# Reordering copies for the transposing DMA: from ScalarE and VectorE to GpSimd

## The chip, the core and the metric

The kernel runs on one core of a Trainium2 chip. A core has a matrix engine (TensorE, PE in the profile; its weight loads are PEld), three engines for elementwise work (VectorE or DVE, ScalarE or ACT, GpSimd or POOL), an engine that mostly issues transfers (SyncE, SP), and 16 DMA engines that move data between the device memory and the on-chip memory SBUF, or within SBUF. Matmuls write into PSUM, here one tile of 8 banks. Each engine works through its own instructions in order and waits on semaphores for the others. The metric is the device time of one execution in microseconds; lower is better.

## What is computed

Attention with a squared ReLU in the place of the softmax, and then a two-layer feed-forward net with a parametric ReLU over the same tokens:

```python
# q, k, v: (8, 12, 448, 64) float32
scores = (1 / sqrt(64)) * q @ k^T
attn   = maximum(scores, 0) ** 2 / 448
x      = (attn @ v).transpose(0, 2, 1, 3).reshape(3584, 768)
h      = x @ w_in                       # w_in: (768, 2048)
g      = maximum(h, 0) + alpha * minimum(h, 0)
out    = g @ w_out                      # w_out: (2048, 768), out: (3584, 768) float32
```

## The kernel before

The work is cut into 24 quads. A quad is four heads of one batch, so there are three quads to a batch (NG = 3); quad n belongs to batch n // 3. The 448 rows of a sequence are taken as 64 times 7: row 7 * pp + j lies on partition pp, and j runs from 0 to 6. On the other 64 partitions lies the second head of a pair, and the index m (called s later) tells two such pairs apart. All tiles that TensorE reads are bfloat16.

A quad goes through these steps:

- **Load.** `load_qk(n)` and `load_v(n)` (L111 to L125) issue one transfer each for q, k and v on GpSimd's queue, which also turns float32 into bfloat16. q and k arrive as raw tiles of 128 partitions by (s, j, d), 896 elements. There are three raw buffers for q, three for k and six for v.
- **Order and turn.** The score matmul needs q and k with the head dimension on the partitions. The first five quads are turned on TensorE (`turn_pe`). From quad 5 on `turn_dma` (L188) does it: two copies (L195), one for q and one for k, put the raw rows from the order (s, j, d) into (j, s, d) in a tile `perm`, and one transposing DMA on SP's queue (L197) makes the tile T of the quad from it. The pool of `perm` has one buffer; that of T has four. For quads 5, 7 and 8 the copies go to the tile `w_mix`, which is not yet in use for its own purpose.
- **Wait and load on.** `prepare(n)` (L408) calls `turn_dma(n)` and then `land(n)` (L417), a copy of one element on GpSimd that reads T. It holds up GpSimd's queue until T(n) is there; behind it stand the loads of q and k for quad n + 2 and of v for quad n + 1.
- **Scores.** For each j, `score_mm` (L209) makes four 64 by 64 matmuls into a pair of PSUM banks. ReLU goes from PSUM to SBUF on ACT (L218) or DVE (L220), the square from SBUF to SBUF on DVE (L231, both inputs the same SBUF tile) or ACT (L229).
- **Attention times v.** `attnv` (L241), 28 matmuls, with the result copied out by ACT (L253) and DVE (L255) into xT.

The feed-forward net runs one batch later. A word f of the plan (`f1_mm`, `f1_out`) is six matmuls over 448 columns (L275) for one of 16 blocks of the hidden dimension, then ACT's negative part (L281) and DVE's combination (L282) into gT. The second layer goes by pairs of 128-row blocks: `Pair` (L315) makes seven products of half size (L335) in the place of eight, with operand sums on DVE (L331, two SBUF inputs, and once L313 for the weights) and output sums on DVE (L340, one input in PSUM); a few blocks go plainly (L300). SP stores the results (L291) out of six output buffers.

There is no scheduler. The order of everything is written out by hand in plans, strings of words that `Walk.step` carries out one by one: f is a block of the first layer, c a chunk of scores with a letter for each ReLU's engine, s a square, v an attention step, p and r steps of a pair, and n the preparation of the next quad. After n stands the engine of its two copies: `nD` is VectorE, a plain `n` is ScalarE. Five plans cover batches 2 to 7; `EACH` serves batches 3, 4 and 6. Plan words that name quads 24 and 25 do nothing. The words n make quads 11 to 23.

Of the kernel before, what the change touches and what calls it, by code (L numbers as in the profile page):

```python
# [20 lines left out]
def kernel(  # L21
# [10 lines left out]
    nc = tc.nc  # L32
    B, H, S, D = q.shape
# [75 lines left out]
    raw, vraw = {}, {}  # L109
# [78 lines left out]
    def turn_dma(n, eng="A"):  # L188
        if n in (5, 7, 8):
            w = w_mix[2 + n % 2].rearrange("p k c -> p (k c)")[:, :4 * NJ * D]  # L190
            p = w.rearrange("p (a j s d) -> p a j s d", a=2, j=NJ, s=2)
        else:
            p = perm_pool.tile([128, 2, NJ, 2, D], BF16, tag="perm", name="perm")
        for i, name in enumerate("qk"):
            (nc.vector.tensor_copy if eng == "D" else nc.scalar.copy)(p[:, i], raw.pop((n, name)).rearrange("p s j d -> p j s d"))  # L195
        t = T_pool.tile([128, 2, NJ, 128], BF16, tag="T", name="T")
        nc.sync.dma_start_transpose(out=t.rearrange("p a j c -> p (a j) c"),  # L197
                                    in_=p.rearrange("p a j s d -> p (a j s d)"))
        T[n] = t
# [208 lines left out]
    def prepare(n, eng="A"):  # L408
        if n < NQ:
            turn_dma(n, eng)  # L410
            land(n)
        if n + 2 < NQ:
            load_qk(n + 2)
        if n + 1 < NQ:
            load_v(n + 1)
# [4 lines left out]
    class Walk:  # L420
# [12 lines left out]
        def step(self, w):  # L433
# [36 lines left out]
            elif c in "pr":  # L470
                if rest[0] in "abcd":
                    getattr(self, c).mix("abcd".index(rest[0]) + 1)
                else:
                    getattr(getattr(self, c), "p" + rest)()
            elif c == "w":
                i, half = int(rest[0]), int(rest[1])
                weight_mix(i, 4 * half, 4 * half + 4)
            elif c == "g":
                f2(self.b // 2, int(rest[0]), int(rest[1]))
            elif c == "n":  # L480
                prepare(self.quad, rest or "A")
                self.quad += 1
            elif c == "x":
                cast0(int(rest[0]), int(rest[1]), rest[2])
            elif c == "t":
                turn_pe(int(rest[0]), ((rest[1], int(rest[2]), int(rest[3]), rest[4]),))
            elif c == "d":
                turn_dma(int(rest[:-1]), rest[-1])
            elif c == "l":
                land(int(rest))  # L490
            elif c == "L":
                n = [int(x) for x in rest[1:].split(",")]
                {"q": load_qk, "v": load_v, "i": load_w_in, "o": load_w_out}[rest[0]](*n)
            elif c == "i":
                warm(int(rest))
            elif c == "z":
                two_queues.append(1)
            elif c == "b":
                nc.vector.tensor_scalar(beta_sb, alpha_sb, -1.0, 1.0, ALU.mult, ALU.add)
# [8 lines left out]
    pairs = {2: (((0, 5), (0, 6)), ((1, 0), (1, 1))), 3: (((1, 2), (1, 3)), ((1, 4), (1, 5))),  # L508
             4: (((1, 6), (2, 0)), ((2, 1), (2, 2))), 5: (((2, 3), (2, 4)),), 6: (((2, 6), (3, 0)), ((3, 1), (3, 2))),
             7: (((3, 3), (3, 4)), ((3, 5), (3, 6)))}  # L510
    FIRST_PAIR = """B f s1A f s2D s0D s1D n f f s0D f f f f s0D cDA cA f s0D s1A nD pa pb r1 f pc s0A f f f f f f p6 r2 cADA s1D v cAA ra s0D pd cA p7 rb n p5 s2D p4 s0D p3 s1A s0A cADA s2A s0D rc r6 v rd cADA s2D r7 r5 s0A s0D cAAD s0A r4 r3 cA v cAA"""
    EACH = """B f s0D f s0A f n f f f f s2A f s1D cAAA s1D f f s0D f s0A f p1 nD f f r1 f f s1A pc p2 pa r2 ra pb cA vDA s1D s0D cAA p6 s0D pd p7 n cA rc s1A cAA s0D s0A p5 p4 rb p3 cAAD v cAD s1D s1A s3A cA s3A r6 s2A r7 rd r5 s0A cAD r4 s0D r3 cAD v cD cA"""
    ONE_PAIR = """B f f nD s2A s0A s2D f s1D f f f s1D f f s0A f f cAD s1D cA s0D n s0D f f f f f f pc pa g50 pb cADA v p1 cAAA s0A p6 s2D s0A p2 pd p7 s1A p5 n s0A p4 p3 s0D cADA s0D v cAD s1A s2A cD s2A s1D g51 s0D cDAD v cD cA cA"""
    LAST = """B f s0A f f f f s3A s2A s2A f f s2A f f f f f f pc f f s0A f p1 r1 pa pb p2 p6 p7 pd ra p5 rb rc p4 p3 r6 z r7 rd r5 r2 r3 r4e"""
    for b, plan in ((2, FIRST_PAIR), (3, EACH), (4, EACH), (5, ONE_PAIR), (6, EACH), (7, LAST)):
        walk.p, walk.r = ([walk.r] if b == 2 else []) + [Pair(*t) for t in pairs[b][b == 2:]] + [None] * (b == 5)
# [31 lines left out]
```

## Time and profile before

| | |
|---|---|
| median of three runs | 372.95 us (372.71 to 373.54) |
| the profiled execution | 373.66 us |
| its span, first to last instruction | 371.9 us |
| mean granted TensorE clock | 0.995 |
| busy: PE, DVE, ACT, POOL | 362.9, 277.9, 274.7, 72.5 us |

The profiled execution is one more run, with its own time; the span is what the profile's rows cover, and 1.8 us lie around it. Busy time counts the union of an engine's instructions, without waits and without the issue of transfers by ACT and SP. [...]

### The profile page before, as it was taken

Reading aid. Unit: us, or ns where it says so; the run is one execution under the profiler, and the core shown is the slowest. Engines: PE = TensorE matmul, PEld = TensorE weight load, DVE = VectorE, ACT = ScalarE, POOL = GpSimd, SP = SyncE. Lnnn points to the kernel's source line nnn. Section 1 sums busy time; section 2 is a strip of 40 time slices with the busy share of each in tenths; the row PEclk is TensorE's granted clock in tenths of the full one; section 3 lists DMA queues with packets and bytes.
Section 4 is the critical chain, followed back from the end, with each engine's and each line's share of the span. In section 5 each row is a group of like instructions: output and inputs, shape, how many; then the busy total and the mean of one; then the engine's idle time right before and its main releaser. Section 6 shows DMA issues by size and latency. Waiting matters only on the chain.

```text
span 371.9 us, 7878 instructions
## 1 busy us (share of the span) xinstructions
PE 362.9 (98%) x3097; PEld 196.7 (53%) x3097; DVE 277.9 (75%) x445; ACT 274.7 (74%) x406; POOL 72.5 (19%) x120
## 2 busy tenths in 40 slices
PE   7799999999999999999999999999999999999996
PEld 5454564445454565545555455554555455555563
DVE  3989988885968989566887668888849667856653
ACT  4998676877997678885897859967699866964400
POOL 8567150304113222021020220202200000000000
PEclk9899999999999999999999999999999999999999
DMA  9999979998999878455882558727647201220024
GB/s 145 193 204 202 196 120 187 159 167 148 183 173 141 119 118 156 102 85 92 156 150 64 96 81 167 143 59 121 101 95 136 50 2 43 65 65 0 0 64 108
DMA packets 73557, 43.29 MB, mean 116 GB/s; under 512 B 40368, under 2 KB 73008, under 8 KB 73520
## 3 DMA queue, kind: packets, MB, share of 16 engines
q0 software_dynamic: 27136, 22.58, 42.0%
q1 hardware_dynamic: 45712, 19.61, 26.1%
q10 hardware_dynamic: 672, 0.59, 0.5%
q8 instruction: 24, 0.39, 0.4%
q14 instruction: 13, 0.11, 0.1%
HBM read 45.62 MB, written 11.01 MB: 152 GB/s over the span
## 4 chain that ended last, share of the span: by engine, by line
PE 91%; ACT 3%; DVE 2%; DMA 1%; issue 1%; ACTq 0%; DVEq 0%; POOLq 0%
PE psum L275 38%; PE psum L335 30%; PE psum L209 8%; PE psum L241 8%; PE psum L300 6%; DMA kraw<-in_k_dram 1%; ACT rl L218 1%; PE psum L183 1%; DVE gT L282 1%; ACT xT L253 1%; ACT neg L281 1%; DVE w_mix L195 1%; DVE at L231 0%; DVE T L186 0%; DVE osb L340 0%
## 5 line engine op out<-in xcount | busy, mean ns | idle before, releaser
L275 PE MATMUL psum<-xT,w_in_sb 128*128 128x448 bf16 x768 | 150.4, 353 | 0.3 <-DVE gT L282 0.2
L282 DVE SCALAR_TENSOR_TENSOR gT<-neg,beta_sb,psum 128x448 bf16<-128x448 f32 x128 | 85.2, 679 | 43.4 <-ACT neg L281 42.1
L218 ACT ACTIVATE rl<-psum 128x896 bf16<-128x896 f32 x128 | 111.1, 924 | 7.2 <-PE psum L209 5.2
L275 PEld LDWEIGHTS <-w_in_sb 128*128 128x128 bf16 x768 | 73.4, 98 | 73.2 <-issue 6.7
L281 ACT ACTIVATE neg<-psum 128x448 f32<-128x448 f32 x128 | 68.5, 547 | 41.0 <-PE psum L275 32.7
L231 DVE TENSOR_TENSOR at<-rl 128x896 bf16<-128x896 bf16 x105 | 62.1, 618 | 0.5 <-ACT rl L218 0.2
L229 ACT ACTIVATE at<-rl 128x896 bf16<-128x896 bf16 x63 | 58.5, 951 | 0.3
L335 PEld LDWEIGHTS <-S 128*128 128x128 bf16 x384 | 36.7, 98 | 28.4 <-issue 5.3
L335 PE MATMUL psum<-w_mix,S 128*128 128x384 bf16 x288 | 49.8, 326 | 0.2
L220 DVE TENSOR_SCALAR rl<-psum 128x896 bf16<-128x896 f32 x40 | 43.2, 1086 | 8.6 <-PE psum L209 8.1
L209 PE MATMUL psum<-T 64*64 64x448 bf16 x672 | 46.2, 361 | 2.1 <-DVE T L186 1.3
L418 POOL COPY landed<-T 1x1 bf16<-1x1 bf16 x18 | 4.1, 229 | 206.8 <-DMA T<-perm 183.1
L335 PEld LDWEIGHTS <-gT 128*128 128x128 bf16 x296 | 28.3, 98 | 20.2 <-issue 1.8
L241 PE MATMUL psum<-at,vraw 64*64 64x448 bf16 x672 | 36.5, 350 | 0.0
L335 PE MATMUL psum<-w_out_sb,gT 128*128 128x384 bf16 x192 | 34.0, 326 | 0.0
L340 DVE TENSOR_TENSOR osb<-psum,u 128x384 f32<-128x384 f32 (+2 forms) x37 | 20.2, 546 | 12.6 <-PE psum L335 8.2
L209 PEld LDWEIGHTS <-T 64*64 64x64 bf16 x672 | 17.4, 106 | 23.1 <-issue 14.9
L241 PEld LDWEIGHTS <-vraw 64*64 64x64 bf16 x672 | 21.2, 107 | 11.8 <-issue 2.7
L300 PE MATMUL psum<-w_out_sb,gT 128*128 128x256 bf16 (+1 forms) x128 | 22.0, 326 | 0.1
L255 DVE TENSOR_SCALAR xT<-psum 128x448 bf16<-128x448 f32 x24 | 14.9, 622 | 9.2 <-PE psum L241 8.7
L253 ACT ACTIVATE xT<-psum 128x448 bf16<-128x448 f32 x24 | 13.2, 549 | 9.1 <-PE psum L241 8.7
L356 ACT COPY osb<-psum 128x384 f32<-128x384 f32 x12 | 5.8, 479 | 17.4 <-PE psum L335 17.4
(43 smaller groups left out, 239.8 us busy)
## 6 DMA issues: line engine op xcount, KB each, us to landing
out_dram<-osb SPq DMA_DIRECT2D x91, 96.0 KB, 2.3
vraw<-in_v_dram POOLq DMA_DIRECT2D x24, 224.0 KB, 6.6
qraw<-in_q_dram POOLq DMA_DIRECT2D x23, 224.0 KB, 4.1
kraw<-in_k_dram POOLq DMA_DIRECT2D x23, 224.0 KB, 5.3
w_in_sb<-in_moe_w_in_dram POOLq DMA_DIRECT2D x16, 192.0 KB, 8.1
w_out_sb<-in_moe_w_out_dram POOLq DMA_DIRECT2D x4, 512.0 KB, 10.5
w_out_sb<-in_moe_w_out_dram POOLq DMA_DIRECT2D x4, 256.0 KB, 8.8
out_dram<-osb SPq DMA_DIRECT2D x8, 128.0 KB, 3.6
```

Of the source, the lines that this page charges most:

```text
L209: nc.tensor.matmul(ps[64 * c:64 * c + 64, r, :S], t[64 * r:64 * r + 64, 1, j, 64 * c:64 * c + 64], t[64 * r:64 * r + 64, 0, :, 64 * c:64 * ...
L218: nc.scalar.activation(rl, ps[:, :, :S], ACTF.Relu)
L220: nc.vector.tensor_scalar(rl, ps[:, :, :S], 0.0, None, ALU.max)
L229: nc.scalar.activation(a, rl, ACTF.Square)
L231: nc.vector.tensor_tensor(a, rl, rl, ALU.mult)
L241: nc.tensor.matmul(ps[64 * s:64 * s + 64, r, :S], vv[64 * r:64 * r + 64, s, j, :], a[64 * r:64 * r + 64, s], start=(j == 0), stop=(j == NJ ...
L275: nc.tensor.matmul(ps, w_in_sb[:, km // 2, km % 2, bass.ts(ff, 128)], xT[b][:, km // 2, km % 2, :], start=(km == 0), stop=(km == KM - 1))
L281: nc.scalar.activation(neg, ps, ACTF.Relu, scale=-1.0)
L282: nc.vector.scalar_tensor_tensor(gT[:, ff, (b % 2) * S:(b % 2) * S + S], neg, beta_sb[:, ff:ff + 1], ps, ALU.mult, ALU.add)
L300: nc.tensor.matmul(ps, gT[:, ff, bass.ts(c, 128)], w_out_sb[:, ff, first_col + lo:first_col + hi], start=(ff == 0), stop=(ff == KF - 1))
L335: nc.tensor.matmul(ps, left[:, i], right[:, i], start=(start and i == 0), stop=(i == KH - 1), skip_group_check=not start)
L340: nc.vector.tensor_tensor(t, ps, u, ALU.add)
```

## The change

In the plans for batches 2 to 6 each word `n` and `nD` becomes `nP`, and `turn_dma` takes a third engine for its copies: GpSimd. Quads 5 to 10, which the words d of the earlier plans turn, keep their engines. The order on PE and SP is the same as before. On ACT 18 copies are gone (quads 11, 13, 14, 16, 17, 19, 21, 22, 23), on DVE 8 (quads 12, 15, 18, 20). On POOL the 26 copies stand behind the loads that follow `land(n - 1)` and ahead of `land(n)`.

```diff
         for i, name in enumerate("qk"):
-            (nc.vector.tensor_copy if eng == "D" else nc.scalar.copy)(p[:, i], raw.pop((n, name)).rearrange("p s j d -> p j s d"))
+            {"D": nc.vector.tensor_copy, "A": nc.scalar.copy, "P": nc.gpsimd.tensor_copy}[eng](p[:, i], raw.pop((n, name)).rearrange("p s j d -> p j s d"))
...
-    FIRST_PAIR = """B f s1A f s2D s0D s1D n f f s0D f f f f s0D cDA cA f s0D s1A nD pa pb r1 f pc s0A f f f f f f p6 r2 cADA s1D v cAA ra s0D pd cA p7 rb n p5 s2D p4 ...
+    FIRST_PAIR = """B f s1A f s2D s0D s1D nP f f s0D f f f f s0D cDA cA f s0D s1A nP pa pb r1 f pc s0A f f f f f f p6 r2 cADA s1D v cAA ra s0D pd cA p7 rb nP p5 s2D p4 ...
-    EACH = """B f s0D f s0A f n f f f f s2A f s1D cAAA s1D f f s0D f s0A f p1 nD f f r1 f f s1A pc p2 pa r2 ra pb cA vDA s1D s0D cAA p6 s0D pd p7 n cA rc ...
+    EACH = """B f s0D f s0A f nP f f f f s2A f s1D cAAA s1D f f s0D f s0A f p1 nP f f r1 f f s1A pc p2 pa r2 ra pb cA vDA s1D s0D cAA p6 s0D pd p7 nP cA rc ...
-    ONE_PAIR = """B f f nD s2A s0A s2D f s1D f f f s1D f f s0A f f cAD s1D cA s0D n s0D f f f f f f pc pa g50 pb cADA v p1 cAAA s0A p6 s2D s0A p2 pd p7 s1A p5 n s0A ...
+    ONE_PAIR = """B f f nP s2A s0A s2D f s1D f f f s1D f f s0A f f cAD s1D cA s0D nP s0D f f f f f f pc pa g50 pb cADA v p1 cAAA s0A p6 s2D s0A p2 pd p7 s1A p5 nP s0A ...
```

More of the change, by code (lines that the diff above doesn't have):

```diff
@@ L510 @@
              7: (((3, 3), (3, 4)), ((3, 5), (3, 6)))}
-    FIRST_PAIR = """B f s1A f s2D s0D s1D n f f s0D f f f f s0D cDA cA f s0D s1A nD pa pb r1 f pc s0A f f f f f f p6 r2 cADA s1D v cAA ra s0D pd cA p7 rb n p5 s2D p4 s0D p3 s1A s0A cADA s2A s0D rc r6 v rd cADA s2D r7 r5 s0A s0D cAAD s0A r4 r3 cA v cAA"""
-    EACH = """B f s0D f s0A f n f f f f s2A f s1D cAAA s1D f f s0D f s0A f p1 nD f f r1 f f s1A pc p2 pa r2 ra pb cA vDA s1D s0D cAA p6 s0D pd p7 n cA rc s1A cAA s0D s0A p5 p4 rb p3 cAAD v cAD s1D s1A s3A cA s3A r6 s2A r7 rd r5 s0A cAD r4 s0D r3 cAD v cD cA"""
-    ONE_PAIR = """B f f nD s2A s0A s2D f s1D f f f s1D f f s0A f f cAD s1D cA s0D n s0D f f f f f f pc pa g50 pb cADA v p1 cAAA s0A p6 s2D s0A p2 pd p7 s1A p5 n s0A p4 p3 s0D cADA s0D v cAD s1A s2A cD s2A s1D g51 s0D cDAD v cD cA cA"""
+    FIRST_PAIR = """B f s1A f s2D s0D s1D nP f f s0D f f f f s0D cDA cA f s0D s1A nP pa pb r1 f pc s0A f f f f f f p6 r2 cADA s1D v cAA ra s0D pd cA p7 rb nP p5 s2D p4 s0D p3 s1A s0A cADA s2A s0D rc r6 v rd cADA s2D r7 r5 s0A s0D cAAD s0A r4 r3 cA v cAA"""
+    EACH = """B f s0D f s0A f nP f f f f s2A f s1D cAAA s1D f f s0D f s0A f p1 nP f f r1 f f s1A pc p2 pa r2 ra pb cA vDA s1D s0D cAA p6 s0D pd p7 nP cA rc s1A cAA s0D s0A p5 p4 rb p3 cAAD v cAD s1D s1A s3A cA s3A r6 s2A r7 rd r5 s0A cAD r4 s0D r3 cAD v cD cA"""
+    ONE_PAIR = """B f f nP s2A s0A s2D f s1D f f f s1D f f s0A f f cAD s1D cA s0D nP s0D f f f f f f pc pa g50 pb cADA v p1 cAAA s0A p6 s2D s0A p2 pd p7 s1A p5 nP s0A p4 p3 s0D cADA s0D v cAD s1A s2A cD s2A s1D g51 s0D cDAD v cD cA cA"""
     LAST = """B f s0A f f f f s3A s2A s2A f f s2A f f f f f f pc f f s0A f p1 r1 pa pb p2 p6 p7 pd ra p5 rb rc p4 p3 r6 z r7 rd r5 r2 r3 r4e"""
```

## The prediction, made before the changed kernel ran

> **What bounds the kernel now.** I read the page's busy shares first, then the same shares cut at the batches, then the waits.
>
> ```profile
> PE 362.9 (98%) x3097; PEld 196.7 (53%) x3097; DVE 277.9 (75%) x445; ACT 274.7 (74%) x406; POOL 72.5 (19%) x120
> ```
>
> Busy time by stretch (window and its length, then busy time and count of PE, PEld, DVE, ACT, POOL, then clock, DMA share, GB/s):
>
> ```profile
> 110.00:153.00 43.00, 42.94 (x360) 23.21 (x358) 36.04 (x59) 32.91 (x49) 10.45 (x17) 1.00 0.88 146
> 153.00:199.00 46.00, 45.94 (x380) 24.52 (x376) 33.26 (x54) 38.09 (x56) 6.99 (x12) 1.00 0.63 112
> 199.00:245.00 46.00, 45.94 (x381) 24.53 (x377) 34.44 (x55) 37.38 (x55) 6.99 (x12) 1.00 0.61 110
> 245.00:287.00 42.00, 42.00 (x356) 22.70 (x352) 32.53 (x50) 33.66 (x51) 5.55 (x10) 1.00 0.59 103
> ```
>
> These four stretches hold the whole change (the last copies that move, of quad 23, are at 291.2 us, just behind the fourth). TensorE is idle 0.18 us in 177. The view of waits, cut to 110:332, names no wait of PE at all. So PE is a wall: relieving ScalarE and VectorE can give back only what stalls are hidden in the starts of matmuls. Matmuls of L275 start every 189 ns throughout (excess over the median 0.7 us in the whole run). The visible stalls after 110 us are four of 0.13 us (first product after the batch's last attention, at 144.98, 189.64, 235.59 and 323.58), one of 0.29 us at 286.72 and some 0.1 us besides: 0.9 us. That is the ceiling of any gain. What can move the time is a new PE stall.
>
> **Removed.** Of quads 11 to 23, nine pairs leave ScalarE and four leave VectorE:
>
> ```profile
> L195 ACT COPY perm<-qraw x11: 938/950/964, 92.3 to 291.2; 128x896 bf16<-128x896 bf16 x11
> L195 ACT COPY perm<-kraw x11: 947/961/974, 93.1 to 292.0; 128x896 bf16<-128x896 bf16 x11
> L195 DVE COPY perm<-qraw x5: 609/612/614, 61.7 to 248.7; 128x896 bf16<-128x896 bf16 x5
> L195 DVE COPY perm<-kraw x5: 607/609/610, 62.3 to 249.2; 128x896 bf16<-128x896 bf16 x5
> ```
>
> ACT: 9 x (0.950 + 0.961) = 17.2 us less work; DVE: 4 x (0.612 + 0.609) = 4.9 us less. (Two ACT pairs and one DVE pair of these rows belong to quads 6, 9 and 10 and stay.) Both lie beside PE, so they are worth nothing by themselves, only room.
>
> **Added: the 26 copies on POOL.** The trace has no 896-element copy there. Its rows are
>
> ```profile
> L418 POOL COPY landed<-T x18: 176/176/647, 49.5 to 297.2; 1x1 bf16<-1x1 bf16 x18
> masks.py:199 POOL TENSOR_SCALAR_AFFINE_SELECT ident<-ident 128x128 bf16<-128x128 bf16 x1 | 0.3, 287 | 0.1
> ```
>
> 128 elements in 287 ns against one element in 176 ns is 0.87 ns per element, so 176 + 895 x 0.87 = 0.96 us a copy, 1.9 us a pair, 25.0 us in all. Lower end: VectorE's 0.61 us. Upper end: seven times the 287 ns row, 2.0 us. I take 0.96, because its slope comes from an operation with one input and one output on this engine.
>
> [...]
>
> **Moved: when they run.** POOL's queue gives the start. After the one-element copy that waits for T of quad n-1 (0.18 us, idle 0.33) come three load issues of 0.72 us, then the copies of quad n: 2.8 us after T(n-1) landed. Quad 11: 111.15 + 2.8 = 113.9 to 115.9, where ScalarE made it from 112.8 to 114.6. The raw rows were loaded one quad earlier, so no wait for them. The transpose is issued by SP at 115.9 instead of 114.6, the landing (7.8 us later, as before) at some 123.7; quad 12 copies at 126.5 to 128.4 (before 122.9 to 124.0), quad 13 near 139 to 141 (before 137.7 to 139.5). T(12) then lands near 137 and is first read at 147.7; T(13) near 147, read at 162.5. From quad 14 on the copies are ready long before SP gets to them: T(14) stands behind a store that SP issues at 152.3, T(17) behind one at 198.0, T(20) behind 244.1, T(23) behind 285.4, so T lands up to 7 us earlier than now. The lead stays 10 us or more everywhere (12 or more now). Behind SP's wait stand the stores, at worst those after T(13): issued from 141.2 now, some 1.3 us later then; their six output buffers leave several us. POOL's one-element copies and loads queue behind the new copies, but they wait for T anyway. I cost all of this at nothing; without the lead, each late T would stop PE for its lateness.
>
> **The cost: the port.** The one-element copy on POOL takes 0.18 us, but longer three times. Two of them (start, duration):
>
> ```profile
> 122.37 0.62 DVE L231 TENSOR_TENSOR at<-rl 128x896 bf16<-128x896 bf16 x1
> 122.38 0.65 POOL L418 COPY landed<-T 1x1 bf16<-1x1 bf16 x1 [7.86 <-DMA T<-perm]
> ...
> 99.44 0.61 DVE L231 TENSOR_TENSOR at<-rl 128x896 bf16<-128x896 bf16 x1
> 99.69 0.41 POOL L418 COPY landed<-T 1x1 bf16<-1x1 bf16 x1 [11.21 <-DMA T<-perm]
> ```
>
> Each ends 0.04 us after L231, a VectorE operation with two inputs in SBUF; the third (0.42 at 49.46, beside an L231 from 49.22) does the same. Beside L282, L220 and L340, with at most one tensor input in SBUF, it takes 0.18. So POOL waits out a two-input DVE operation. Whether DVE waits out a POOL copy no row shows: from zero to the whole remaining copy. I take the whole, as the mirror of the rows. [...]
>
> How often: the two-input operations between 110 and 332 us are
>
> ```profile
> L231 DVE TENSOR_TENSOR at<-rl 128x896 bf16<-128x896 bf16 x54 | 32.4, 618 | 0.1
> L331 DVE TENSOR_TENSOR S<-gT 128x1024 bf16<-128x1024 bf16 x18 | 11.7, 683 | 0.0
> L331 DVE TENSOR_TENSOR S<-S,gT 128x1024 bf16<-128x1024 bf16 x9 | 6.2, 685 | 0.1
> L331 DVE TENSOR_TENSOR S<-gT,S 128x1024 bf16<-128x1024 bf16 x9 | 6.1, 683 | 0.0
> ```
>
> 90 in 222 us, 0.405 per us. In 25.0 us of copying about 10 start, and wait 0.48 us on average: 4.9 us of DVE delay, by chance as much as DVE sheds. Queued behind the waiting operation are L282, L340, L220 and L255, which empty the PSUM banks PE writes next. How much of a delay reaches PE I reckoned by going back from PE's start times through waits and queues in the trace: the room behind the 73 two-input operations up to 290 us has quartiles 0.29, 0.53 and 1.07 us, a tenth has 0.16 or less. The narrow ones are where output sums follow the mixes: at 186.88 L340 empties a bank in 0.56 us that PE's L241 takes at 187.49. A wait uniform from 0 to 0.96 exceeds a room r by (0.96 - r)^2 / 1.92 on average: 0.33, 0.16, 0.02 and 0 us for rooms 0.16, 0.41, 0.75 and over 1, mean 0.13. Ten of them: 1.3 us; two at one spot (three L231 in a row stand at 113.56, where quad 11 falls) make it a little more, the relief of ACT a little less. I take 1.4 us. With 0.61 us a copy the same working gives 6.4 waits and 0.35 us; with 2.0 us, 21 waits x 0.48 = 10 us.
>
> **Sum.** The profiled execution took 373.66 us (span 371.9 and 1.8 around it), the median of the runs is 372.95, 0.7 below. 373.66 + 1.4 = 375.0 for such an execution, 374.3 for the median.
>
> **Rivals.**
> - *Nothing to measure.* The waits fall into DVE's idle time (31.4 us before L282 between 110 and 332) or DVE does not wait. For: median room is over the mean wait. Against: a tenth of the spots have no room and PE has no spare time to catch up with. 372.9.
> - *Faster.* With ScalarE free of 1.9 us ahead of the batch's end, evictions come sooner and the 0.9 us of small PE stalls goes; it decides if fewer than three copies meet a tight L231 or L331 (three at 0.33 us cost the 0.9 again). Against: at 144.39 ACT stood idle 0.51 us before the eviction that PE waited for, so its queue was not the cause. 372.05.
> - *Long copies.* Over 1.5 us each; then 10 us of stalls: 383. Above some 2.2 us a copy, T(n-1) to T(n) takes 2.8 + 4.4 + 8 = 15.2 us, as long as a quad (three in 46 us), the lead shrinks, and T itself comes late. For: nothing of this size was seen on POOL. Against: the slope of 0.87 ns.
> - *It doesn't do what it says.* Excluded: the 26 copies stand in POOL's order, PE's and SP's orders are unchanged.
>
> **How the numbers follow.** A measurement of this kernel tells apart about 0.2%, 0.75 us. Forecast (+0.8 to +7, most likely +1.4): 52%. Nothing to measure: 30%. Faster: 8%. Long copies: 10%. So slower 0.62, same 0.30, faster 0.08. The range runs from 372.5 (the faster case cut in half) to 380 (copies of some 1.6 us), leaving out most of the long copies and part of the faster case.
>
> **What would show it.** Right: POOL L195 rows near 960 ns, longer where they meet L231; L231's or L331's longest well over 0.63 and 0.69, or gaps before them, only beside POOL copies; PE waits on DVE between 113 and 285 us adding up to 1 to 2 us; ACT near 257 us busy. Wrong: L231 unchanged beside a copy (no lock on this side), POOL rows of 1.5 us or more, PE waiting for T, or a PE row as full as now.

## The result, and the profile after

The changed kernel takes 376.02 us (median of six runs, 375.11 to 377.10) against 373.20 us of before on the same chip: the ratio is 1.0075, with a 95% interval of 1.0059 to 1.0090. It is slower by 2.8 us, 0.75%. In a second comparison, beside other runs of before ("whole again" below), the ratio was 1.0079 (1.0057 to 1.0102). The forecast of 374.3 us had the sign and the mechanism, and half the size.

The profiled execution took 375.63 us with a span of 373.9. From its page, the busy shares and the first line of the chain that ended last (before, that chain had PE 91% and DVE 2%):

```profile
PE 363.3 (97%) x3097; PEld 197.2 (53%) x3097; DVE 279.6 (75%) x437; ACT 261.0 (70%) x388; POOL 97.9 (26%) x146
PE 87%; DVE 8%; ACT 3%; issue 1%; ACTq 0%; DVEq 0%
```

ACT lost 13.7 us of busy time and eight operations are gone from DVE, yet DVE is busier than before by 1.7 us. Without 4.9 us of copies it should have shown 273. The missing 6.6 us stand in operations that did not change. Before:

```profile
L231 DVE TENSOR_TENSOR at<-rl x105: 615/618/627, 8.9 to 329.4; 128x896 bf16<-128x896 bf16 x105
L331 DVE TENSOR_TENSOR S<-gT x24: 679/684/693, 94.0 to 359.2; 128x1024 bf16<-128x1024 bf16 x24
L331 DVE TENSOR_TENSOR S<-S,gT x12: 681/683/692, 95.8 to 358.6; 128x1024 bf16<-128x1024 bf16 x12
```

After, with GpSimd's copies:

```profile
L231 DVE TENSOR_TENSOR at<-rl x105: 611/619/1820, 8.5 to 330.8; 128x896 bf16<-128x896 bf16 x105
L331 DVE TENSOR_TENSOR S<-gT x24: 679/685/1418, 93.1 to 360.6; 128x1024 bf16<-128x1024 bf16 x24
L331 DVE TENSOR_TENSOR S<-S,gT x12: 681/689/1501, 94.8 to 360.0; 128x1024 bf16<-128x1024 bf16 x12
L195 POOL COPY perm<-qraw x13: 947/962/1065, 112.3 to 283.2; 128x896 bf16<-128x896 bf16 x13
L195 POOL COPY perm<-kraw x13: 919/957/1430, 113.2 to 284.1; 128x896 bf16<-128x896 bf16 x13
```

The columns after the count are shortest, median and longest in ns. The medians of L231 and L331 are as before; the longest are two to three times as long. Eleven such rows are longer than normal, by 6.6 us together, and each has a GpSimd copy beside it. The reverse holds as well: no two-input row that lies beside a copy kept its usual time, and all 24 other VectorE rows beside a copy, with at most one tensor input in SBUF, did. So the wait is counted into the row of the operation that waits. The prediction and the expectations call this a lock on a port, and a hold is the time for which one GpSimd operation lasts. What the traces show is the longer rows; no run shows a port.

What reaches TensorE is in the view of waits of PE, cut to 108:335, which was empty between 110 and 332 us before:

```profile
PE psum L241 <- DVE osb L340: 0.5, 1, 0.5
PE psum L209 <- DVE rl L220: 0.4, 1, 0.4
PE psum L275 <- DVE gT L282: 0.4, 1, 0.4
PE psum L209 <- DVE u L340: 0.3, 1, 0.3
```

That is 1.6 us of visible waits. PE's order is the same in both kernels, so each matmul's start can be set against its start before. From the first matmul after 105 us to the last it took 262.9 us before and 265.2 us after, 2.3 us more. PE falls behind in four steps of 0.4 to 0.6 us, at 119.3, 144.7, 234.1 and 288.1 us, and by 0.3 us in smaller ones. The rest of the difference between the two profiled executions is not the change's: the start was 0.9 us quicker in this one and the stretch behind the last matmul 0.6 us longer. In a second profile of the changed kernel, an execution of 376.39 us, PE loses 2.8 us over the same stretch.

One step in full, from the timeline (start, duration):

```profile
231.37 0.73 POOL L124 DMA_DIRECT2D vraw<-in_v_dram  x1
231.42 1.46 PE L335 MATMUL psum<-w_out_sb,S 128*128 128x384 bf16 x8
...
232.08 0.96 POOL L195 COPY perm<-qraw 128x896 bf16<-128x896 bf16 x1
232.10 1.50 DVE L331 TENSOR_TENSOR S<-S,gT 128x1024 bf16<-128x1024 bf16 x1
...
232.95 1.43 POOL L195 COPY perm<-kraw 128x896 bf16<-128x896 bf16 x1
...
233.52 0.55 DVE L340 TENSOR_TENSOR osb<-psum,u 128x384 f32<-128x384 f32 x1
...
234.12 1.52 PE L241 MATMUL psum<-at,vraw 64*64 64x448 bf16 x28 [0.54 <-DVE osb L340]
```

GpSimd's copy of quad 20's q rows starts 0.02 us ahead of the operand sum L331. L331 ends at 233.60, 0.56 us after the copy's end at 233.04, so it waited the copy out, 0.8 us. The output sum L340 queues behind it and empties the PSUM banks that the attention step L241 takes: PE idles 0.54 us. This is one of the tight places that the prediction named (186.88 us, one batch earlier). The second copy, of the k rows, in turn waited for L331: it shows 1.43 us.

### The profile page after: what moved, and what is told of

It reads as the page before. It is cut to its first block, busy times and chain, and to the rows that moved or that the text cites. A ratio compares the mean times of both kernels' runs of the same rounds, so it can differ in the third digit from the quotient of the medians.

```text
span 373.9 us, 7835 instructions
## 1 busy us (share of the span) xinstructions
PE 363.3 (97%) x3097; PEld 197.2 (53%) x3097; DVE 279.6 (75%) x437; ACT 261.0 (70%) x388; POOL 97.9 (26%) x146
## 4 chain that ended last, share of the span: by engine, by line
PE 87%; DVE 8%; ACT 3%; issue 1%; ACTq 0%; DVEq 0%
PE psum L275 35%; PE psum L335 29%; PE psum L241 8%; PE psum L209 8%; PE psum L300 5%; DVE at L231 2%; DVE gT L282 2%; DVE rl L220 2%; PE psum L165 1%; ACT neg L281 1%; PE psum L183 1%; DVE S L331 1%; ACT rl L218 1%; DVE w_mix L195 1%; ACT xT L253 1%
## 5 line engine op out<-in xcount | busy, mean ns | idle before, releaser
L231 DVE TENSOR_TENSOR at<-rl 128x896 bf16<-128x896 bf16 x105 | 65.6, 651 | 0.5 <-ACT rl L218 0.2
L335 PEld LDWEIGHTS <-S 128*128 128x128 bf16 x384 | 36.6, 98 | 28.2 <-issue 5.1
L335 PE MATMUL psum<-w_mix,S 128*128 128x384 bf16 x288 | 49.8, 326 | 0.2
L335 PEld LDWEIGHTS <-gT 128*128 128x128 bf16 x296 | 28.3, 98 | 20.2 <-issue 1.8
L241 PE MATMUL psum<-at,vraw 64*64 64x448 bf16 x672 | 36.7, 350 | 0.6 <-DVE osb L340 0.5
L335 PE MATMUL psum<-w_out_sb,gT 128*128 128x384 bf16 x192 | 34.0, 326 | 0.0
L340 DVE TENSOR_TENSOR osb<-psum,u 128x384 f32<-128x384 f32 (+2 forms) x37 | 20.2, 546 | 12.2 <-PE psum L335 8.9
L241 PEld LDWEIGHTS <-vraw 64*64 64x64 bf16 x672 | 21.1, 106 | 12.8 <-issue 3.8
L117 POOL DMA_DIRECT2D qraw<-in_q_dram x23 | 16.6, 722 | 6.5 <-issue 3.4
```

Source lines behind the costliest of these rows:

```text
L231: nc.vector.tensor_tensor(a, rl, rl, ALU.mult)
L241: nc.tensor.matmul(ps[64 * s:64 * s + 64, r, :S], vv[64 * r:64 * r + 64, s, j, :], a[64 * r:64 * r + 64, s], start=(j == 0), stop=(j == NJ ...
L335: nc.tensor.matmul(ps, left[:, i], right[:, i], start=(start and i == 0), stop=(i == KH - 1), skip_group_check=not start)
L340: nc.vector.tensor_tensor(t, ps, u, ALU.add)
```

## The experiments

All times are medians beside runs of the kernel before on the same chip (373.2 to 373.4 us). The line numbers of their kernels are up to four higher than those above: L235, L234 or L232 is then the square L231, and L335, L334 or L332 the operand sum L331.

### The copies added, nothing moved

Two copies for each of quads 11 to 23 are added to the kernel before; `used` keeps every raw tile after its own copies have read it:

```diff
-            raw[(n, name)] = t
+            raw[(n, name)] = used[(n, name)] = t
...
+        if n >= 11:
+            for name in "qk":
+                spent = used[(n - 1, name)].rearrange("p s j d -> p j s d")
+                nc.gpsimd.tensor_copy(spent, spent)
         for i, name in enumerate("qk"):
             (nc.vector.tensor_copy if eng == "D" else nc.scalar.copy)(p[:, i], ...
```

> The kernel before, with all its ScalarE and VectorE copies kept, and beside them two GpSimd copies of 896 elements for each of quads 11 to 23, at the same place in GpSimd's queue as in the changed kernel. They rewrite in place the raw tiles of the quad before, which nobody reads any more: 25 us of GpSimd work that no other engine waits for. Lock theory (a GpSimd copy holds the SBUF port, and a VectorE operation with two SBUF inputs waits for its end): L231 and L331 rows beside the copies grow to 1.0 to 1.8 us, 4 to 8 us in all, and the time rises by 1 to 4 us (374.2 to 377), though T is neither early nor late. Rival, moved work (the loss comes from T, from SP's order or from the changed order on ScalarE and VectorE): L231 stays at 0.62 us and the time is that of before within 0.5 us.

Measured: 379.44 us, ratio 1.0159 (1.0137 to 1.0180), 6.1 us slower. That is beyond what the lock theory had allowed, and far from the rival's 0.5 us. From the first matmul after 105 us to the last it took 269.3 us, 6.4 more than before. ScalarE and VectorE do all that they did, T arrives by the old way, and nobody uses or waits for the added results. The rows of the two-input operations and one meeting:

```profile
L235 DVE TENSOR_TENSOR at<-rl x105: 606/617/1873, 8.8 to 335.2; 128x896 bf16<-128x896 bf16 x105
L335 DVE TENSOR_TENSOR S<-gT x24: 678/686/3041, 93.4 to 365.0; 128x1024 bf16<-128x1024 bf16 x24
```

```profile
176.54 4.24 DVE L335 TENSOR_TENSOR S<-gT 128x1024 bf16<-128x1024 bf16 x3
...
177.08 0.73 POOL L124 DMA_DIRECT2D vraw<-in_v_dram  x1
177.80 0.96 POOL L197 COPY qraw<-qraw 128x896 bf16<-128x896 bf16 x1
...
178.67 0.96 POOL L197 COPY kraw<-kraw 128x896 bf16<-128x896 bf16 x1
...
181.44 0.34 PE L339 MATMUL psum<-w_mix,S 128*128 128x384 bf16 x1 [1.50 <-DVE S L335]
```

Three sums that take some 2 us took 4.24; one of them shows 3.04 us, through both copies, and PE idles 1.50 us for the sums. The loss is made by GpSimd's copies alone, not by what they replace. That it is twice the changed kernel's has two sides that this run does not part: the copies met other operations (15 long rows, 12.5 us together), and VectorE and ScalarE still carried the copies that the change takes from them.

### The same, but only writing

```diff
-                nc.gpsimd.tensor_copy(spent, spent)
+                nc.gpsimd.memset(spent, 0.0)
```

> As the kernel with extra copies (the kernel before, all its copies kept, 26 extra GpSimd operations on raw tiles that nobody reads any more), but each extra operation only writes: a fill of 896 elements in the place of a copy, some 0.9 us by the slope of the 128-element fill (223 ns against 100 ns for one element). It asks which part of the port is held. If a two-input VectorE operation collides only with a GpSimd operation that reads SBUF: L231 and L331 stay at 0.62 and 0.68 us and the time is that of before within 0.7 us (372.7 to 374.1). If any GpSimd operation collides: again 3 us or more, 376.5 to 380.

Measured: 373.10 us, ratio 0.9998 (0.9983 to 1.0012). The fills take nearly as long as the copies (0.86 against 0.96 us) and stand at the same place in the queue. Twenty-one two-input operations overlap a fill, and none of them is longer than usual by more than 0.01 us:

```profile
L197 POOL MEMSET qraw<- x13: 864/864/872, 113.7 to 282.1; 128x896 bf16 x13
L235 DVE TENSOR_TENSOR at<-rl x105: 609/617/631, 8.5 to 328.9; 128x896 bf16<-128x896 bf16 x105
L335 DVE TENSOR_TENSOR S<-gT x24: 674/682/692, 93.5 to 358.7; 128x1024 bf16<-128x1024 bf16 x24
```

So it is not GpSimd's load, its queue or its writes that hold VectorE up. What a copy has and a fill has not is its read. No run here has a GpSimd operation that only reads, so that the read alone does it is not shown.

### Relief without any copy

```diff
-            p = perm_pool.tile([128, 2, NJ, 2, D], BF16, tag="perm", name="perm")
+            p = kept_perm[0] if n >= 12 else perm_pool.tile([128, 2, NJ, 2, D], BF16, tag="perm", name="perm")
...
-            {"D": nc.vector.tensor_copy, "A": nc.scalar.copy, "P": nc.gpsimd.tensor_copy}[eng](p[:, i], ...
...
+            if n < 12:
+                {"D": nc.vector.tensor_copy, "A": nc.scalar.copy, "P": nc.scalar.copy}[eng](p[:, i], src)
```

> The changed kernel with the copies of quads 12 to 23 left out; quad 11 has ScalarE make them, and the later transposes turn the same ordered rows again, so scores of the later quads are wrong. It shows what the relief of ScalarE and VectorE is worth without any GpSimd copy. Lock theory and the reading that PE is the bound: nothing beyond the small PE stalls can be won, 372.3 to 373.3. Rival (relief pays, and the lock hid it): 371.5 or less. If the loss came from the relief or the new order itself, the time stays at 375 or more.

Measured: 373.69 us, ratio 1.0009 (0.9994 to 1.0024); the median is 0.4 us above the band, the interval holds no change. From the first matmul after 105 us to the last it took 262.87 us, as before (262.88). Taking 20 us of work from ScalarE and VectorE (eight pairs of 1.91 us, four of 1.22) wins nothing, and the new order without the copies loses nothing. So relief of this kind has nothing to give beyond the noise, wherever the copies are put.

### Four quads back, and four quads only

```diff
     def turn_dma(n, eng="A"):
+        eng = {11: "A", 14: "A", 20: "D", 23: "A"}.get(n, eng)
```

> The changed kernel with only quads 11, 14, 20 and 23 given back to ScalarE (11, 14, 23) and VectorE (20); nine pairs stay on GpSimd. In the trace of the changed kernel the four steps by which PE falls behind (0.4 to 0.6 us each, 2.2 us together) follow the copies of these four quads. Lock theory: those four steps go, and the time falls to within 0.8 us of before (373 to 374), unless the copies of other quads move onto a pair of two-input operations. Rival, a cost spread over all 26 copies or the moved work: 9/13 of the loss stays, 1.9 us, 375.1.

Measured: 374.55 us, ratio 1.0024 (0.9998 to 1.0049), 1.2 us over before; the interval just holds no change. The four steps are gone, and two others have come, 0.3 us near 186 and 0.5 us near 267: the copies of the remaining quads run elsewhere now. PE loses 1.0 us in the profiled execution. Ten two-input rows are long (5.0 us together), and PE waits where it did not in the changed kernel:

```profile
PE psum L210 <- DVE rl L221: 0.4, 1, 0.4
PE psum L242 <- DVE osb L341: 0.3, 1, 0.3
```

The time lies between the two expectations, above the first's band of 373 to 374 with the exception it allowed for, and below the even share of 375.1.

```diff
     def turn_dma(n, eng="A"):
+        if n >= 11 and n not in (11, 14, 20, 23):
+            eng = "D" if n in (12, 15, 18) else "A"
```

> The counterpart of the run with four quads given back: only quads 11, 14, 20 and 23 are copied on GpSimd, the other nine stay on ScalarE and VectorE as before. Lock theory: these four made the four steps of PE in the changed kernel, some 2 us, less where the copies fall otherwise: 374.3 to 376.3. Rival, a cost spread evenly: 4/13 of the loss, 0.9 us, 374.2 or less.

Measured: 375.61 us, ratio 1.0055 (1.0035 to 1.0074), 2.4 us over before. Four of thirteen pairs make most of the loss; the even share of 0.9 lies below the interval, which is 1.3 to 2.8 us. So the cost goes by what stands beside each copy and not by the count. The two losses, 1.2 and 2.4, add up to more than 2.8, but the intervals are too wide to make anything of that. The profiled execution (374.33 us) was the fastest of the seven: it has three long rows, and PE loses 0.8 us in it. What makes the rest of the 2.4 us in the slower ones no trace shows.

### Length of one hold

The same bytes in 7 pieces a copy, and in two:

```diff
...
+            for j in range(NJ if eng == "P" else 1):
+                copy(p[:, i, j:j + 1] if eng == "P" else p[:, i], src[:, j:j + 1] if eng == "P" else src)
```

> The changed kernel with each GpSimd copy cut into 7 copies of 128 elements (one for each j), 182 in the place of 26. Lock theory: what counts is how long one copy holds the port; a piece of some 0.25 us holds up a VectorE operation by 0.25 us at most each time, mostly inside the room it has, so the PE stalls shrink to under 0.5 us in all and the time comes within 0.7 us of before (372.8 to 373.9), although GpSimd is busier (some 3.5 to 4 us a pair). Rival, the load on the port counts and not the length of one hold: more GpSimd time gives the same or a larger loss, 376 or more.

Measured: 373.89 us, ratio 1.0025 (1.0004 to 1.0046). From the first matmul after 105 us to the last it took 262.87 us, what it took before: in the profiled execution (373.33 us) PE loses nothing. Four of the twelve executions took 375.2 to 376.8 us, and none of those was profiled. GpSimd is busier than with whole copies, 121.7 against 97.9 us, so GpSimd's busy time is not what counts:

```profile
L198 POOL COPY perm<-qraw x91: 279/315/782, 111.8 to 284.1; 128x128 bf16<-128x128 bf16 x91
L334 DVE TENSOR_TENSOR S<-gT x24: 679/685/3070, 93.3 to 358.5; 128x1024 bf16<-128x1024 bf16 x24
```

Most of the 18 long rows are long by 0.1 to 0.2 us. The worst is not: an L334 at 124.08 us took 3.07 us, while ten pieces went by in a row. Here short pieces did not let the other engine in. This one stood among the first layer's blocks, where PE did not wait for it.

```diff
...
+            for lo, hi in ((0, 4), (4, NJ)) if eng == "P" else ((0, NJ),):
+                copy(p[:, i, lo:hi], src[:, lo:hi])
```

> The changed kernel with each GpSimd copy cut in two (512 and 384 elements), 52 copies of some 0.6 and 0.5 us. It stands between the whole copies (0.96 us, 2.8 us slower than before) and the sevenths (0.3 us, about 0.5 us slower). If the loss goes by the length of one hold: some 1 to 1.8 us, 374.3 to 375.1, and single two-input VectorE rows of 1.1 to 1.3 us where the whole copies made 1.3 to 1.8. If cutting helps only because some conflict of phase goes by chance: anything, 373.3 or 376 as well.

> The changed kernel itself, on the chip and beside the runs of before that the halved copies are compared with, so that the series of whole, half and seventh has its first point on the same scale: 375.5 to 376.5, 2.8 us over before. A run near 374 would say that the loss depends on the chip or the phase more than on the copies.

Measured: halves 375.25 us, ratio 1.0049 (1.0031 to 1.0066); the changed kernel again 376.38 us, ratio 1.0079 (1.0057 to 1.0102); before 373.28. By their medians whole copies cost 3.1 us, halves 2.0 and sevenths 0.5, and in the profiled executions PE loses 2.8, 1.6 and 0.0 us. The order is that of the length of one hold, by the medians 0.96, 0.6 and 0.3 us. Whole copies and sevenths are clearly apart; the interval of the halves overlaps both others, and the sevenths were measured on another chip. The halves are 0.15 us above their band, and their longest two-input row, 1.61 us through several halves in a row, is above the 1.1 to 1.3 us expected.

### Another place, and another neighbour

The first edit puts the two copies ahead of the three load issues. The second has the order load q, copy q, load k, copy k, load v. The core of both edits (the second also takes one load from the list `ahead` before each copy):

```diff
-        if n + 2 < NQ:
-            load_qk(n + 2)
-        if n + 1 < NQ:
-            load_v(n + 1)
+        if n + 2 < NQ:
+            ahead.extend([lambda: load_qk(n + 2, "q"), lambda: load_qk(n + 2, "k")])
+        if n + 1 < NQ:
+            ahead.append(lambda: load_v(n + 1))
...
+        while ahead:
+            ahead.pop(0)()
         t = T_pool.tile([128, 2, NJ, 128], BF16, tag="T", name="T")
```

> The changed kernel with one thing moved: in GpSimd's queue the two copies of a quad stand ahead of the three load issues that now precede them, so they run 2.2 us earlier relative to the landing of the T before; nothing is added or taken away. Lock theory: only what VectorE does at that moment counts, so the loss changes with the shift, by 1 us or more either way, between 373.3 and 379, and the steps by which PE falls behind stand where L231 or L331 meets a copy. Rival, the loss comes from copies or T being late: 2.2 us earlier gives the time of before, 373.4, with no PE step; a cost that goes by the count of copies stays at 376.

Measured: 375.68 us, ratio 1.0054 (1.0033 to 1.0075). Most pairs now start as soon as the T before has landed, where they stood 2.4 us behind it, and the loss is nearly the same: the rival of late copies falls. The lock theory's sharp part, a change of 1 us or more, fails too, since the loss went from 2.8 to 2.4. But two of the pairs that cost most have hardly moved: quad 11's starts at 112.62 us (112.34 in the changed kernel), 3.2 us behind its landing in both, and quad 14's at 142.40 (142.58), since T(13) landed 2.1 us later. Two of the three steps of PE in this trace stand behind them. By time alone this run does not tell the lock from a cost by count. Its long rows stand where copies now stand (a new pair at 259.45 and 260.51 us).

> The changed kernel with GpSimd's queue reordered to load q, copy q, load k, copy k, load v, so that 0.72 us of load issue, beside which L231 never grew in the trace of before, stands between the two copies of a quad. Lock theory with a pair that holds the port as one (L231 waited 1.82 us through two copies in the changed kernel, L331 3.04 us with the extra copies): no two-input row over 1.7 us, at most one copy is waited for, and the loss is smaller, 373.6 to 375.4. Rival, the pair does not matter: about the loss of the changed kernel, 375.5 to 376.5, only at other places.

Measured: 376.10 us, ratio 1.0066 (1.0043 to 1.0089). The expectation was wrong in both its parts: the loss is that of the changed kernel, and two rows pass 1.7 us. (The 1.82 and 3.04 us that it names are whole rows; the waits in them are 1.20 and 2.36 us.)

```profile
L335 DVE TENSOR_TENSOR S<-gT x24: 674/685/2380, 93.2 to 361.8; 128x1024 bf16<-128x1024 bf16 x24
L335 DVE TENSOR_TENSOR S<-S,gT x12: 674/683/1904, 94.9 to 361.2; 128x1024 bf16<-128x1024 bf16 x12
```

The load issue of 0.72 us between the two copies did not part them: both rows last into the second copy, by 0.49 and 0.21 us. The last section comes back to this.

## Why the prediction was right, and where its size was off

- **PE is the bound and relief is worth nothing: right.** Leaving the copies out altogether changed neither the time (1.0009, 0.9994 to 1.0024) nor the stretch from 105 us on.
- **The copy's price: right.** 0.96 us was forecast, 962 and 957 ns are the medians. ACT's busy time fell by 13.7 us, not 17.2. Added up row by row it fell by 16.2, since other rows grew by 1.0. The rest is overlap: rows overlap at their ends (a pair of 0.95 and 0.96 us lasted 1.8), and busy time is their union.
- **T is never late: right.** T landed earlier than before for every quad but 22 (282.0 against 281.4 us), by 3.7 us for quad 12 and 8.0 for quad 18. The forecast had T later for quads 12 and 13 (137 and 147 us); they landed at 129.4 and 140.0. It counted 7.8 us from the issue of a transpose to its landing; the trace after has 5.2 us for quad 11 and 4.4 for quad 12. Why they are quicker no run shows, and T had no part in the loss.
- **The lock works both ways: right.** That was an assumption from the mirror of three rows (0.41 to 0.65 us for a one-element copy of 0.18). The extra copies show VectorE's side, with rows of up to 3.04 us where 0.68 is usual; beside the fills no row grew by more than 0.01 us.
- **Number of meetings: right, in part by luck.** Ten were forecast to start beside a copy; eleven rows are long, eight that start inside a copy's row and three that start ahead of one. Where the same number of copies fell otherwise, nine rows were long (copies ahead of loads) or fifteen (extra copies).
- **Wait per meeting: too small.** The prediction took a wait as uniform up to one copy, 0.48 us on average and 4.9 us in all. The rows show 0.60 on average, 0.75 for the eight that start inside a copy, up to 1.20, and 6.6 us in all. The waits are not uniform: four of the eight start right behind another two-input operation and near the start of a copy's hold, and wait 0.62 to 0.73 us, most of a copy. One operation waited through two copies. And three rows show a wait (0.08 to 0.33 us) ahead of the copy's row.
- **Share that reaches PE: too small.** It took 1.3 of 4.9 us (27%) to get past the room in front of PE; the trace has 2.3 of 6.6 (35%). The room was reckoned for a single wait at each place. In the trace quad 11's two copies delay two of three L231 in a row by 0.55 and 0.73 us, and three of the pairs (quads 11, 12 and 14) meet two or three two-input operations each. The text named that train and gave it only "a little more".

So the profiled execution lost 2.3 us in the place of 1.4; the second profile lost 2.8, which is also what the medians say. Rival by rival: no change and faster are refuted by the interval; long copies by their rows. What would have been wrong by the prediction's own test (L231 unchanged beside a copy, PE waiting for T) did not appear.

One part stays open: why the extra copies cost 6.1 us, twice as much as the change. ScalarE and VectorE had no room from copies taken away there, and the added copies fell at other moments; both point that way, and no run parts them.

## What to carry to other kernels

Before moving an elementwise operation to GpSimd, look at what VectorE runs beside it. Here GpSimd's copies from SBUF to SBUF held up VectorE's operations with two SBUF inputs, by up to 1.20 us in the changed kernel and 2.36 with the extra copies, and the row of the operation that waited grew while its engine looked busy. With TensorE busy for 98% of the span before the change and its operands ready by some tenths of a microsecond, GpSimd's spare time wasn't free (2.8 us lost), and ScalarE's relief wasn't gain (ratio 1.0009 with the copies left out, an interval that holds no change). Short pieces cost less than long ones here (0.5 against 3.1 us), and fills of nearly the same length cost nothing (ratio 0.9998).

## What was not expected of the hardware

**The wait begins before the copy's row.** In the changed kernel's timeline:

```profile
186.05 1.01 DVE L331 TENSOR_TENSOR S<-S,gT 128x1024 bf16<-128x1024 bf16 x1
186.07 0.73 POOL L124 DMA_DIRECT2D vraw<-in_v_dram  x1
...
186.78 1.06 POOL L195 COPY perm<-qraw 128x896 bf16<-128x896 bf16 x1
```

At its usual 0.68 us L331 would have ended at 186.73, ahead of the copy's start; it took 1.01. The same was counted in other profiles, over the two-input operations that lie more than 0.1 us beside a load issue after 105 us and do not start beside an earlier copy. Over the changed kernel's two profiles and those with extra copies, four quads back, copies between loads and halves, 19 of the 24 whose load issue has a copy right behind it are long (with sevenths, none of 5). Beside load issues with no copy right behind them, in the profiles of before, after and all experiments but the one without copies, none of 108 is long; 12 of these have a fill right behind the issue. So the long rows go with the copy queued behind the load issue, not with the issue by itself. What makes the wait start ahead of the copy's row no run shows.

**The wait isn't bounded by one GpSimd operation.** One L231 waited 1.20 us beyond its own time through two copies of 0.95 us, and an L334 2.4 us through ten pieces of 0.28 us, while other rows got in after the first. By the prediction's reckoning, at most the 0.96 us of one copy, such a wait would end with the first copy. What decides when the waiting operation goes on is open.
